# Loading k by two transfers, and leaving the second product of two blocks instead of four to the last phase, in a fused attention and feed-forward kernel

## The chip, the cores and the metric

The kernel runs on one core of one Trainium2 chip. Its engines each run their own in-order stream of instructions: TensorE (PE, matmuls, with its weight loads shown as PEld), VectorE (DVE), ScalarE (ACT), GpSimd (POOL) and SyncE (SP), whose queue issues nearly all of this kernel's DMAs. The metric is the device time of one execution in microseconds, the median of several runs. A profile is of one execution, and its "span" runs from the first to the last instruction.

## The reference

```python
def _attn_ref(q, k, v, f):                      # q, k, v: (8, 8, 576, 64); f: (8, 8, 576)
    scores = (1.0 / np.sqrt(D)) * np.matmul(q, k.transpose(0, 1, 3, 2))
    cum = np.cumsum(np.log(np.clip(f, 0.0001, 1.0)), axis=-1)
    scores = np.where(causal, -1000000000.0, scores + cum[..., :, None] - cum[..., None, :])
    attn = softmax of scores
    return np.matmul(attn, v)

def reference(...):
    x = attn_out.transpose(0, 2, 1, 3).reshape(B * S, H * D)     # 4608 tokens x 512
    h = x @ w_in                                                 # 512 x 2048
    g = np.maximum(h, 0.0) + np.log1p(np.exp(-np.abs(h)))        # softplus
    return g @ w_out                                             # 2048 x 512
```

So: causal attention with a cumulative decay for 8 batches of 8 heads, each with 576 tokens of 64 values, then a two-layer feed-forward network over the 4608 tokens. Below, "first product" is x @ w_in and "second product" is g @ w_out.

## The kernel before

**Numbers in two parts.** Most matmuls run on pairs: a value is cast to a high part in the engine's rounded float32 type, the rest (value minus high part) is the low part, and a product is high x high + high x low + low x high. So nearly every operand costs a cast (the copies recorded at L327, on ACT or DVE) and a subtraction (on DVE or POOL).

**Attention.** The eight heads of batch 0 are cut in 14 jobs in plain float32 (they fill the first stage, while weights are loaded). The other 56 heads (batches 1 to 7) are one job each, a "whole head". A whole head loads q, k and v (`load`, L881 to L895, and `load_v`), prepares them (`prepare`, L912: decay rows by DMA at L920 and L923, high parts of q and k by L927, low parts by L930 and L931), computes five tiles of scores (`stat_tile`: matmuls L976 and L977, row minimum L981, shift L1018, exponential L1025 on ACT), sums and scales (L1038 to L1055), turns the weights by matmuls into four banks (L1118) and splits them (L1137, L1140), and multiplies by v (L1265) into two banks that are put into x (L1315).

q and k are stored transposed: 64 rows of 576 values for each head. The kernel wants each in all 128 partitions, that is, twice. q is loaded by two transfers, one into partitions 0 to 63 and one into 64 to 127 (L886, 144 KB each). k is loaded by one transfer (L891, 288 KB) whose source pattern begins with a dimension of size 2 and stride 0, so that the 64 rows are read twice. Both go to buffers of the tag `raw`, of which there are two (L371); they alternate, and a buffer comes free when the cast and the subtraction that read it are done.

**Feed-forward blocks.** The first 2560 tokens are seven blocks (L360): 0 and 1 of 128 tokens, 2 of 256, and 3 to 6 of 512. A block's first product runs in 16 units (L1506, 12 matmuls of 512 columns each in a 512-token block), each followed by a softplus on ACT (`gate`, L1536). What comes then depends on the block. Blocks 0 and 1 run in plain float32 (L1485, L1618), and the sums of their second product hold one PSUM bank of tag `att` each. For block 2, the softplus tile is split into high and low parts (L1547, L1551) and multiplied by w_out straight away (`down_part`, L1608, matmuls in `products`, L1599) into two PSUM banks of the tag `att`. There are eight banks: two of tag `h` for the first product, six of tag `att` shared by scores, turned weights, outputs and these sums. For the blocks named in `LATE_DOWN` (3, 4, 5 and 6) the softplus tile is stored raw to DRAM (`raw_m`, two DMAs at L1567), and their second product waits for the last phase. A 512-token block that is not named there takes a third way, which no block takes before: the second product of its first two tiles of 128 tokens runs as units finish, the split parts of the other two tiles are stored (`keep`, L1555), and when the first two are done they are loaded again (`second`, L1646) and multiplied.

**The last phase.** The last 2048 tokens are two super-blocks of 1024, whose first product uses a scheme of seven products of halves in place of eight (L2071). After it comes the second product, by the same scheme, in "sets" of 42 matmuls of 256 columns: load (L2325), sums (L2345), splits (L2379), products (L2412). First the blocks of `LATE_DOWN` (8 sets each: 2 parts of 256 tokens x 4 quarters), then the super-blocks (16 sets each).

**The order.** The whole program is laid out when it is built. Each operation is added to a plan with the engines that can do it, an estimated cost, what it must follow and which buffers it takes. `Plan.run` (L205) then picks, again and again, the operation that can start first by these estimates, chooses its engine and emits it. That fixes each engine's stream; on the chip an instruction waits until what it needs is there, and everything behind it on its engine waits too. Two tables bend the choice: `SOONER` (L52) gives a kind of operation a head start in us, `RATHER` (L102) makes an engine look cheaper or dearer for a kind. Units of feed-forward work are dealt out between the units of attention (`run_ffn`, L2618) by a budget; in most whole heads a unit is dealt only once the budget has reached `PAIR` (L2739), 1.4 us, so they come in pairs.

Of the kernel before, what the change touches and what calls it, by code (L numbers as in the profile page):

```python
# [40 lines left out]
DELAY = 2  # L41
STEPB = -0.3
DEEP = 1
LATE_DOWN = (3, 4, 5, 6)
WSUMB = 0.0
DOWNB = 0.0
PAIR = 1.4

W_FROM, W_EACH = 0, 3
S_FROM, S_EACH = 9, 4  # L50

SOONER = {  # L52
    "attention.finish.put": 0.09,
    "attention.finish_stats.scale": -0.26,
    "attention.load.k": 0.17,
    "attention.output_tiled.values": 0.35,
    "attention.prepare.begin": -0.26,
    "attention.split_v.v_hi": -0.28,
    "attention.split_v.v_lo": 4.97,
    "attention.stat_tile.scores": 0.25,  # L60
    "attention.stat_tile.shift": 0.04,
    "attention.stat_tile.sums": 3.52,
    "attention.weights.keep": 0.05,
    "attention.weights.spread": -0.03,
    "decay.split": 6,
    "ffn_block.gate.lo_part": -0.02,
    "ffn_block.gate.whole_keep": -0.23,
    "ffn_block.split_stored.hi_part": 0.04,
    "ffn_block.split_stored.lo_part": 6,
    "ffn_block.split_stored.load": 6,  # L70
    "ffn_block.split_x.hi_part": -0.87,
    "joined.row": 0.28,
    "load_f64.clip": 0.25,
    "load_f64.join": 0.3,
    "load_f64.low": 0.32,
    "load_f64.scale": -0.22,
    "load_f64.sign": 0.32,
    "mark": -0.05,
    "put_out.<lambda>": 0.06,
    "set_rows.begin": -2.95,  # L80
    "split_w_in.keep": -0.52,
    "split_w_out.hi_part": -0.1,
    "store_x.store": -0.39,
    "super_blocks.down_out.keep": -0.06,
    "super_blocks.down_out.sum_.go": -0.2,
    "super_blocks.down_set.<lambda>": -0.67,
    "super_blocks.down_set.split.high": -0.28,
    "super_blocks.down_set.split.low": 0.03,
    "super_blocks.gate.store": -1.45,
    "super_blocks.hold_sums.begin": 5.59,  # L90
    "super_blocks.lay_sums.low": 0.15,
    "super_blocks.lay_w.split.hi": 1.29,
    "super_blocks.lay_w.split.lo": 0.23,
    "super_blocks.lay_w.step.go": 0.13,
    "super_blocks.lay_x.less.go": 0.28,
    "super_blocks.lay_x.split.high": -0.08,
    "super_blocks.lay_x.split.low": 1.61,
    "super_blocks.super_block.product.mm": -1.42,
    "super_blocks.super_block.ups.sum_of.go": 3.23,
    "turn_mask.turn": -1.48,  # L100
}
RATHER = {  # L102
    ("attention.finish_stats.scale", "DVE"): -0.98,
    ("attention.prepare.<lambda>", "ACT"): 0.02,
    ("attention.prepare.<lambda>", "DVE"): -0.18,
    ("attention.weights.hi_part", "DVE"): 1.11,
    ("attention.weights.keep", "ACT"): -1.02,
    ("attention.weights.keep", "DVE"): -1.85,
    ("attention.weights.spread", "ACT"): 0.73,
    ("ffn_block.gate.hi_part", "DVE"): 1.02,  # L110
    ("put_out.<lambda>", "DVE"): 0.72,
    ("split_w_in.hi_part", "DVE"): -1.77,
    ("split_w_out.hi_part", "DVE"): -2,
    ("super_blocks.down_set.split.high", "ACT"): -0.65,
    ("super_blocks.down_set.sum_.<lambda>", "DVE"): -0.83,
    ("super_blocks.lay_sums.<lambda>", "DVE"): -0.15,
    ("super_blocks.lay_sums.high", "ACT"): -1.79,
    ("super_blocks.lay_sums.low", "DVE"): -0.98,
    ("super_blocks.lay_w.split.hi", "DVE"): 1.26,
    ("super_blocks.lay_w.split.lo", "DVE"): -0.29,  # L120
    ("super_blocks.lay_x.split.high", "ACT"): 0.58,
    ("super_blocks.lay_x.split.high", "DVE"): 0.26,
}


def kind_of(emit):

    return emit.__qualname__.split("<locals>.", 1)[-1].replace("<locals>.", "")
# [15 lines left out]
class Plan:  # L144
# [14 lines left out]
    def add(self, on, emit, after=(), takes=(), lag=None, loose=False):  # L159
        op = Op(on, emit, after, takes, lag)  # L160
        op.loose = loose
        kind = kind_of(emit)
        op.sooner = SOONER.get(kind, 0.0)
        if len(op.on) > 1:
            op.on = [x._replace(bias=x.bias + RATHER.get((kind, x.eng), 0.0)) for x in op.on]
        op.at = len(self.ops)
        op.rank = op.at + self.late
        self.ops.append(op)
        for t in set(takes):
            self.queue[t].append(op)  # L170
        for d in op.after:
            d.users.append(op)
        return op

    def give(self, tag, ops):

        left = [len(ops), 0.0]
        for op in ops:
            self.gives.setdefault(op, []).append((tag, left))
# [78 lines left out]
def on_pe(n, times=1, m=128):  # L258

    return On("PE", times * (max(n * 0.000444, m * 0.00092) + 0.002))  # L260
# [20 lines left out]
def on_dma(kb, n=1, eng="SP"):  # L281

    return On(eng, max(0.6 * n, kb / RATE) if eng == "SP" else 1.5 * n)


def dma_lag(kb, n=1, eng="SP"):
    each = 0.6 if eng == "SP" else 1.5
    return each * (n - 1) + 2.1 + kb / n / RATE - on_dma(kb, n, eng).cost
# [26 lines left out]
def last_first(x, n=64):  # L315

    *lead, (_, w) = x.ap
    return bass.AP(x.tensor, x.offset + w - n, [*lead, [-n, w // n], [1, n]])
# [12 lines left out]
def tile_decay_attention_softplus_ffn(  # L331
# [39 lines left out]
                x32=2, ps=2, wl=2, vhl=3, vraw=1, raw=2, one=2)  # L371
    plan = Plan(BUFS | dict(T0=4, stat=4, p=2, xh0=1, xh1=1, xl0=1))
    add, give = plan.add, plan.give

    def joined():
        parts = []

        def row(e):
            for part in parts:
                part(e)  # L380

        op = add(On("PE", 0.0), row)
        op.parts = parts
        return op
# [11 lines left out]
    def add_dma(emit, kb, n=1, eng="SP", **more):  # L396
        return add(on_dma(kb, n, eng), emit, lag=dma_lag(kb, n, eng), **more)
# [9 lines left out]
    def buf(tag, shape, name, dtype=F32):  # L407
        return pool.tile(shape, dtype, tag=tag, name=name, bufs=BUFS[tag])
# [39 lines left out]
    raw_d = dpool.tile([NSUPER, 2, 2, SUPER // 256, 2, P, NFP // 2, P], F32, name="raw_d")  # L448
    raw_m = dpool.tile([len(LATE_DOWN), 2, 2, WIDE // 256, 2, P, NFP // 2, P], F32, name="raw_m")
    kept_at = {}  # L450
# [51 lines left out]
    def exchange(e):  # L502
# [12 lines left out]
            lambda e, x=x, v=v: e.mul(x, ident[0:BH, 0:BH], v) if e is nc.scalar  # L515
# [261 lines left out]
    def attention(job):  # L777

        b, heads = job["b"], job["heads"]
# [29 lines left out]
        st = {}  # L809
# [71 lines left out]
        def load():  # L881
            def q(e):
                st["q"] = buf("raw", [P, S], f"q{n}")
                for r in (0, 64):
                    out = st["q"][r : r + 64].rearrange("p (n t) -> p n t", t=64)
                    e.dma_start(out=out, in_=last_first(qkT[b, :, heads[0], 0]))  # L886

            def k(e):
                st["k"] = buf("raw", [P, S], f"k{n}")
                x = qkT[b, :, heads[0], 1]  # L890
                e.dma_start(out=st["k"], in_=bass.AP(x.tensor, x.offset, [[0, 2], *x.ap]))  # L891

            st["ql"] = add_dma(q, 288, 2, takes=("raw",))
            st["kl"] = add_dma(k, 288, takes=("raw",))

        def split_v():
            def v_hi(e):
# [427 lines left out]
        def loads():  # L1325
            if quad:
                load_quad()
            elif pair:
                st["T"] = T_of[heads[0]]
                st["vr"], st["V"], st["vtag"] = V_of[heads[0]]  # L1330
            else:
                (load32 if plain else load)()
                load_v()
# [53 lines left out]
    def ffn_block(i):  # L1387
# [148 lines left out]
        def gate(u):  # L1536
# [23 lines left out]
            give("h", [a])  # L1560
            if i in LATE_DOWN:
                m = LATE_DOWN.index(i)

# [129 lines left out]
        up_t, down_t = on_pe(nt, 6).cost, on_pe(DM, 3 * ahead).cost  # L1693
        raw_only = i in LATE_DOWN
        if plain:
# [33 lines left out]
    def super_blocks():  # L1729
# [704 lines left out]
        def down_out(s, k, out_box):  # L2434
# [4 lines left out]
            else:  # L2439
                t0 = BLOCKS[LATE_DOWN[s - NSUPER]][0]  # L2440
                rows = out[t0 : t0 + WIDE].rearrange("(t n) d -> t n d", t=2)
# [64 lines left out]
        sets = [  # L2506
            (NSUPER + m, k, q) for m in range(len(LATE_DOWN)) for k in range(WIDE // 256) for q in range(NQ)
        ]
# [109 lines left out]
    def run_ffn(budget, least=0.0):  # L2618
        if budget < least:
            return budget  # L2620
        while ffn and budget > 0:
            cost, unit = ffn.pop(0)
            plan.late = FFN_RANK
            unit()
            plan.late = 0
            budget -= cost
        return budget
# [49 lines left out]
    for n in range(len(jobs) + 1):  # L2677
# [58 lines left out]
        for unit in units:  # L2736
            unit()
            steady = n > nstart + H and (n - nstart) % H in (2, 3, 4, 5, 6)
            credit = run_ffn(credit + share, PAIR if steady else 0.0)  # L2739
        old = cur  # L2740
# [59 lines left out]
```

## Time and profile before

| | |
|---|---|
| three runs | 1365.43, 1368.46, 1370.01 us; median 1368.46 |
| the profiled execution | 1367.31 us, span 1365.2 us, mean granted TensorE clock 0.926 |
| busy in the span | PE 1185.0 us (87%), DVE 1011.4 (74%), ACT 813.7 (60%), POOL 387.1 (28%) |
| DMA | 204.83 MB, mean 150 GB/s; queue 1 takes 51.0% of 16 engines' time |
| HBM | 143.27 MB read, 59.93 MB written |

How to read the profile: its first part gives each engine's busy time; the second cuts the span in 40 equal slices with the busy share of each in tenths, the granted TensorE clock (PEclk) in tenths, and the DMA engines' mean busy share. The chain of waits is followed back from the last instruction: at each step to what released it. Groups of instructions are listed by source line, engine and tiles, as "out<-in", with count, busy time, mean ns of one, and the idle time of the engine just before them with what ended it. A line can be that of a helper: L327 is every copy and cast. A busy PE is not PE at its peak, since matmuls overlap and their ends are modelled: a matmul of 512 columns is shown as some 0.4 us long, while in a dense run the starts lie closer. The windows view gives the busy time of each engine in a stretch of the span, in us, with the number of instructions.

### The profile page before, as it was taken

How to read it: one execution, taken by the hardware profiler on the slowest of the kernel's cores; microseconds unless marked ns; L12 is line 12 of the kernel's file. 1: busy time of each engine (PE TensorE's matmuls, PEld its weight loads, DVE VectorE, ACT ScalarE, POOL GpSimd, SP SyncE). 2: the span in 40 equal slices, each digit the busy share in tenths (PEclk: the TensorE clock that was granted, in tenths of full speed). 3: DMA queues.
4: the chain of work that ended last, by engine and by line, in shares of the span. 5: the costliest groups of instructions: out<-in, count | busy, mean ns of one | idle time of the engine just before them, and what ended most of it. 6: DMA issues, size and time to landing. Idle time of an engine off the chain costs nothing.

```text
span 1365.2 us, 23032 instructions
## 1 busy us (share of the span) xinstructions
PE 1185.0 (87%) x7328; PEld 1029.5 (75%) x7328; DVE 1011.4 (74%) x2813; ACT 813.7 (60%) x2020; POOL 387.1 (28%) x356
## 2 busy tenths in 40 slices
PE   9998878788876678778777778999999999999998
PEld 7766667676765567566666567888788999999998
DVE  8997677667767476656665666765989988888884
ACT  6765756567766656666656667655666444444442
POOL 3334343234333343333433243021341111011010
PEclk9999888788888688987988898999999999999999
DMA  7875455344444334444444445787765444444442
GB/s 223 258 209 167 128 159 157 109 126 118 139 132 131 98 104 126 136 126 134 125 132 129 133 123 173 248 219 231 217 204 163 138 133 121 135 139 131 125 133 70
DMA packets 240058, 204.83 MB, mean 150 GB/s; under 512 B 85088, under 2 KB 208256, under 8 KB 239936
## 3 DMA queue, kind: packets, MB, share of 16 engines
q1 hardware_dynamic: 239912, 203.34, 51.0%
q8 instruction: 58, 0.95, 0.3%
q14 instruction: 64, 0.52, 0.1%
q10 hardware_dynamic: 24, 0.02, 0.0%
HBM read 143.27 MB, written 59.93 MB: 149 GB/s over the span
## 4 chain that ended last, share of the span: by engine, by line
PE 44%; DMA 33%; DVE 9%; ACT 5%; POOL 3%; issue 3%; SPq 2%; POOLq 0%; ACTq 0%; DVEq 0%
DMA k<-in_qkT 27%; PE late_E L2412 11%; PE late_E L2071 5%; PE late_B L2412 3%; PE late_D L2412 3%; PE late_C L2412 3%; PE late_A L2412 3%; PE h L1506 3%; POOL T L931 2%; DMA vr<-in_vR 2%; ACT T L327 2%; DMA wi_d<-woh_dt_float 2%; PE late_C L2071 2%; PE late_D L2071 2%; PE b L1118 1%
## 5 line engine op out<-in xcount | busy, mean ns | idle before, releaser
L976 PE MATMUL s<-T 128*128 128x192 f32 (+1 forms) x336 | 110.9, 340 | 76.9 <-DVE pl L1140 31.6
L1265 PE MATMUL o<-ph,vhl 128*128 128x512 f32 x336 | 108.8, 346 | 70.6 <-ACT p L1025 66.3
L931 POOL TENSOR_TENSOR T<-k,T 64x576 fp32r<-64x576 f32 x56 | 80.5, 1438 | 284.1 <-ACT T L327 142.9
L1025 ACT ACTIVATE pb<-s,negm 128x288 f32<-128x288 f32 (+5 forms) x272 | 142.6, 527 | 23.2 <-DVE negm L1018 19.5
L981 DVE CUSTOM_DVE_ANT_0 s<-s,cmask 128x448 f32<-128x448 f32 (+6 forms) x320 | 134.3, 445 | 23.6 <-PE s L977 19.3
L1265 PEld LDWEIGHTS o<-ph,vhl 128*128 128x128 f32 x336 | 74.4, 225 | 90.0 <-ACT p L1025 78.0
L976 PEld LDWEIGHTS s<-T 128*128 128x128 f32 (+1 forms) x336 | 67.2, 200 | 99.2 <-DVE pl L1140 38.2
L327 ACT CAST T<-k 64x576 fp32r<-64x576 f32 (+1 forms) x91 | 59.4, 671 | 128.0 <-DMA k<-in_qkT 128.0
L1315 DVE TENSOR_TENSOR x<-o,x 64x64 f32<-64x64 f32 x112 | 50.7, 455 | 98.8 <-ACT x L327 97.7
L1140 DVE TENSOR_TENSOR pl<-b,ph 128x512 fp32r<-128x512 f32 x168 | 105.0, 658 | 10.7 <-ACT ph L327 9.5
L977 PE MATMUL s<-T 68*128 68x192 f32 (+1 forms) x336 | 105.6, 318 | 0.0
L327 ACT CAST ph<-b 64x128 fp32r<-64x128 f32 x224 | 100.3, 486 | 6.0 <-PE b L1118 4.9
L1506 PE MATMUL h<-xh,wl 128*128 128x512 f32 (+1 forms) x320 | 101.8, 406 | 0.0
L931 POOL TENSOR_TENSOR T<-q,T 64x576 fp32r<-64x576 f32 x56 | 80.2, 1432 | 59.3 <-PE b L1118 24.6
L1506 PE MATMUL h<-xh,wih 128*128 128x512 f32 (+1 forms) x320 | 92.2, 415 | 1.4 <-ACT xh L327 1.4
L1118 PE MATMUL b<-halves,pb 128*128 128x128 f32 x512 | 91.5, 301 | 0.0
L1506 PE MATMUL h<-xl,wih 128*128 128x512 f32 (+1 forms) x320 | 88.5, 403 | 0.0
L903 POOL TENSOR_TENSOR vhl<-vr,vhl 128x384 fp32r<-128x384 f32 x56 | 56.8, 1015 | 102.5 <-DVE vhl L327 53.4
L1025 ACT ACTIVATE p<-s,negm 128x192 f32<-128x192 f32 (+1 forms) x112 | 40.5, 362 | 66.6 <-DVE negm L1018 66.2
L1265 PE MATMUL o<-pl,vhl 128*128 128x512 f32 x224 | 78.1, 397 | 0.1
L2345 POOL TENSOR_TENSOR fY<-fX,late_ph 128x256 f32<-128x256 f32 x13 | 10.4, 800 | 231.6 <-ACT late_pl L327 142.0
L977 PEld LDWEIGHTS s<-T 68*128 68x128 f32 (+1 forms) x336 | 68.2, 203 | 7.5 <-issue 1.8
(703 smaller groups left out, 3732.5 us busy)
## 6 DMA issues: line engine op xcount, KB each, us to landing
wl<-wil_d SPq DMA_DIRECT2D x40, 512.0 KB
raw_m<-e SPq DMA_DIRECT2D x128, 128.0 KB
raw_d<-e SPq DMA_DIRECT2D x64, 256.0 KB
q<-in_qkT SPq DMA_DIRECT2D x112, 144.0 KB
k<-in_qkT SPq DMA_DIRECT2D x56, 288.0 KB
vr<-in_vR SPq DMA_DIRECT2D x64, 160.0 KB
x_d<-x SPq DMA_DIRECT2D x28, 288.0 KB
late_r<-wi_d SPq DMA_DIRECT2D x14, 512.0 KB
```

The lines of the kernel that those rows point to most:

```text
L327: (e.tensor_copy if hasattr(e, "tensor_copy") else e.copy)(out, in_)
L931: e.tensor_sub(t[rows, i, :], st[x][rows], tb[rows, j, :])
L976: e.matmul(o, qA[:, S - end : S - q0], kA[:, a:z], start=True, stop=False)
L977: e.matmul(o, qB[0:ST, S - end : S - q0], kB[0:ST, a:z], start=False, stop=True)
L981: e.tensor_tensor_reduce(out=box["o"], in0=box["o"], in1=cmask[0:n_q, right - w : right], scale=-0.125, scalar=m0 if i else 3.0e38, op0=AL ...
L1025: e.activation(o, box["o"], AF.Softplus, bias=m1, scale=-1.0, accum_out=acc)
L1118: e.transpose(box["ps"][0 : x.shape[1], at : at + one.shape[1]], x, one)
L1140: e.tensor_sub(box["l"], box["ps"][:, 0:w], box["h"].bitcast(F32))
L1265: e.matmul(boxes[gi]["ps"][0:m, a:z], st["vhl"][:, c, 0:m], pbox[which][:, o : o + z - a], start=gi in fresh and which == "h", stop=gi == ...
L1506: e.matmul(o, l, r, start=m == 0, stop=m == 11)
L2071: e.matmul(banks[to], stationary(x, j), at(b, y, j), start=start and m == 0, stop=m == 5, skip_group_check=not start,)
L2412: e.matmul(like(o, y), x, y, start=q == 0 and f_ == 0 and m == 0, stop=q == NQ - 1 and f_ == 1 and m == 2,)
```

## The change

Three things change.

1. k is loaded by two transfers of 64 rows, as q is, in place of one of 128 rows with a repeating source. The plan is told that it is two.
2. `LATE_DOWN` is (5, 6) in place of (3, 4, 5, 6). Blocks 3 and 4 compute their second product in the middle (the third way above), and the last phase has two blocks fewer.
3. `PAIR` is 0.0 in place of 1.4, and the two tables are new: `SOONER` has 58 entries in place of 48 and `RATHER` 23 in place of 20, nearly all with other values. (`kind` also gets a suffix from an attribute `phase`, which nothing sets.)

```diff
-LATE_DOWN = (3, 4, 5, 6)
+LATE_DOWN = (5, 6)
 WSUMB = 0.0
 DOWNB = 0.0
-PAIR = 1.4
+PAIR = 0.0
...
 SOONER = {
-    "attention.finish.put": 0.09,
-    "attention.finish_stats.scale": -0.26,
-    "attention.load.k": 0.17,
...
+    "attention.finish_stats.scale": -0.13,
+    "attention.load.q": 0.09,
+    "attention.load32.qk": 4.25,
...
 RATHER = {
-    ("attention.finish_stats.scale", "DVE"): -0.98,
-    ("attention.prepare.<lambda>", "ACT"): 0.02,
...
+    ("attention.finish_stats.scale", "ACT"): -0.62,
+    ("attention.finish_stats.scale", "DVE"): -0.94,
...
-        kind = kind_of(emit)
+        kind = kind_of(emit) + getattr(self, "phase", "")
...
             def k(e):
                 st["k"] = buf("raw", [P, S], f"k{n}")
-                x = qkT[b, :, heads[0], 1]
-                e.dma_start(out=st["k"], in_=bass.AP(x.tensor, x.offset, [[0, 2], *x.ap]))
+                for r in (0, 64):
+                    e.dma_start(out=st["k"][r : r + 64], in_=qkT[b, :, heads[0], 1])

             st["ql"] = add_dma(q, 288, 2, takes=("raw",))
-            st["kl"] = add_dma(k, 288, takes=("raw",))
+            st["kl"] = add_dma(k, 288, 2, takes=("raw",))
```

More of the change, by code (lines that the diff above doesn't have):

```diff
@@ L52 @@
 SOONER = {
-    "attention.finish.put": 0.09,
-    "attention.finish_stats.scale": -0.26,
-    "attention.load.k": 0.17,
[L56 to L60, printed above, removed]
-    "attention.stat_tile.shift": 0.04,
[L62 to L72, printed above, removed]
-    "load_f64.clip": 0.25,
[L74 to L81, printed above, removed]
@@ L82 @@
-    "split_w_out.hi_part": -0.1,
-    "store_x.store": -0.39,
[L84 to L100, printed above, removed]
+    "attention.finish_stats.scale": -0.13,
+    "attention.load.q": 0.09,
+    "attention.load32.qk": 4.25,
+    "attention.load32.rows": 3.94,
+    "attention.output_tiled.put": 0.2,
+    "attention.prepare.<lambda>": -0.12,
+    "attention.prepare.decay_rows": 6,
@@ new lines @@
+    "attention.split_v.v_hi": -0.01,
+    "attention.split_v.v_lo": -0.07,
+    "attention.stat_tile.scores": 0.13,
+    "attention.stat_tile.shift": 0.04,
+    "attention.stat_tile.sums": 2.24,
+    "attention.weights.keep": -0.21,
+    "attention.weights.spread": -0.84,
+    "attention.weights.turn": 0.04,
+    "decay.<lambda>": -0.09,
+    "decay.store": 0.98,
+    "ffn_block.gate.hi_part": -0.02,
+    "ffn_block.gate.keep": 0.99,
+    "ffn_block.gate.lo_part": 0.01,
+    "ffn_block.gate.raw": -0.09,
@@ new lines @@
+    "ffn_block.split_stored.hi_part": 0.05,
+    "ffn_block.split_stored.lo_part": 5.53,
+    "ffn_block.split_stored.load": 5.04,
+    "ffn_block.split_x.hi_part": -0.12,
+    "ffn_block.up_part.load": 0.15,
+    "joined.row": 0.25,
+    "load_f64.clip": 0.25,
+    "load_f64.join": 0.17,
+    "load_f64.low": 0.24,
+    "mark": 0.07,
+    "put_out.<lambda>": -0.63,
+    "put_out.begin": -1.19,
+    "set_rows.<lambda>": 0.63,
+    "set_rows.begin": 3.55,
+    "split_w_in.hi_part": 0.03,
+    "split_w_in.keep": -0.37,
@@ new lines @@
+    "split_w_in.lo_part": -0.05,
+    "split_w_out.hi_part": -0.47,
+    "split_w_out.lo_part": -0.09,
+    "store_x.store": -0.39,
+    "super_blocks.down_products.mm": -2.57,
+    "super_blocks.down_set.<lambda>": -1.84,
+    "super_blocks.down_set.split.high": -0.24,
+    "super_blocks.gate.store": -0.66,
+    "super_blocks.lay_out.sums": 0.07,
+    "super_blocks.lay_sums.high": -0.59,
+    "super_blocks.lay_w.<lambda>": -0.92,
+    "super_blocks.lay_w.split.hi": 0.39,
+    "super_blocks.lay_w.split.lo": 3.36,
@@ L101 @@
+    "super_blocks.lay_w.step.go": 0.09,
+    "super_blocks.lay_x.load": -0.26,
+    "super_blocks.lay_x.split.high": -0.15,
+    "super_blocks.lay_x.split.low": 0.29,
+    "super_blocks.super_block.product.mm": -1.71,
+    "super_blocks.super_block.ups.moved.<lambda>": -0.8,
+    "super_blocks.super_block.ups.sum_of.go": -0.08,
+    "turn_mask.turn": -1.39,
 }
 RATHER = {
-    ("attention.finish_stats.scale", "DVE"): -0.98,
-    ("attention.prepare.<lambda>", "ACT"): 0.02,
-    ("attention.prepare.<lambda>", "DVE"): -0.18,
@@ L106 @@
[L106 to L122, printed above, removed]
+    ("attention.finish_stats.scale", "ACT"): -0.62,
+    ("attention.finish_stats.scale", "DVE"): -0.94,
+    ("attention.finish_stats.scale", "POOL"): -0.12,
+    ("attention.prepare.<lambda>", "ACT"): 0.4,
@@ new lines @@
+    ("attention.prepare.<lambda>", "DVE"): 0.26,
+    ("attention.split_v.v_hi", "ACT"): -0.39,
+    ("attention.split_v.v_hi", "DVE"): -1.23,
+    ("attention.weights.hi_part", "DVE"): 0.57,
+    ("attention.weights.keep", "ACT"): -1.5,
+    ("attention.weights.keep", "DVE"): -1.93,
+    ("ffn_block.gate.hi_part", "DVE"): -0.14,
+    ("ffn_block.gate.lo_part", "POOL"): -2,
+    ("load_f64.sign", "POOL"): -0.61,
+    ("set_rows.<lambda>", "DVE"): -2,
+    ("set_rows.<lambda>", "POOL"): -1.65,
+    ("split_w_in.hi_part", "ACT"): 1.76,
@@ L123 @@
+    ("super_blocks.down_set.split.high", "ACT"): 0.19,
+    ("super_blocks.down_set.split.high", "DVE"): -0.18,
+    ("super_blocks.down_set.sum_.<lambda>", "POOL"): 1.41,
+    ("super_blocks.lay_sums.<lambda>", "DVE"): -0.2,
+    ("super_blocks.lay_w.split.hi", "ACT"): 0.13,
+    ("super_blocks.lay_w.split.hi", "DVE"): 0.07,
+    ("super_blocks.lay_x.split.high", "ACT"): -1.28,
 }
```

## The prediction

> **What bounds the kernel now.** I read the page's head and slices first, then the busy time by stage, then the chain of waits of the long stage.
>
> ```profile
> span 1365.2 us, 23032 instructions
> ...
> PE   9998878788876678778777778999999999999998
> ...
> PEclk9999888788888688987988898999999999999999
> ```
> ```profile
> core 0: us, PE busy (x) PEld busy (x) DVE busy (x) ACT busy (x) POOL busy (x), PEclk, DMA share, GB/s
> 0.00:85.00 85.00, 82.52 (x560) 63.94 (x561) 75.40 (x249) 60.48 (x144) 29.79 (x55) 1.00 0.79 235
> 85.00:867.00 782.00, 613.15 (x3361) 508.25 (x3360) 527.18 (x1730) 510.20 (x1417) 283.08 (x227) 0.87 0.47 136
> 867.00:1059.00 192.00, 187.43 (x896) 155.63 (x895) 153.98 (x284) 110.48 (x214) 44.30 (x46) 1.00 0.73 210
> 1059.00:1365.00 306.00, 301.88 (x2516) 301.67 (x2514) 254.87 (x554) 132.58 (x247) 29.89 (x29) 1.00 0.41 125
> ```
>
> Three of the four stages are full: PE is busy 97%, 98% and 99% of them, at a granted clock of 1.00. The middle (85 to 867 us, the 56 whole heads and the blocks beside them) is not: PE 613.15 of 782 us (78%) at 0.87, DVE 67%, ACT 65%, POOL 36%. No engine fills it, so a chain of waits does. Its shares in that window, three of its pieces (start, length), and who waits for the loads from 85 to 838 us (total, times, longest):
>
> ```profile
> by line: DMA k<-in_qkT 47.9%; POOL T L931 4.2%; issue 3.9%; DMA vr<-in_vR 3.6%; ACT T L327 3.5%; PE h L1506 3.4%; DMA wi_d<-woh_dt_float 3.1%; DVE pl L1140 2.3%; SPq L886 2.2%; DVE s L981 2.1%; PE o L1265 2.0%; DMA sto<-in_w_out 2.0%; PE b
> ```
> ```profile
> 537.03 9.04 DMA k<-in_qkT
> 550.41 10.36 DMA k<-in_qkT
> 563.03 9.11 DMA k<-in_qkT
> ```
> ```profile
> ACT T L327 <- DMA k<-in_qkT: 128.0, 37, 5.9
> DVE T L327 <- DMA k<-in_qkT: 66.2, 17, 5.0
> ...
> DVE T L327 <- DMA q<-in_qkT: 2.0, 4, 0.7
> ```
>
> The load of k is 47.9% of 782, 375 us. One takes 9.04 to 10.36 us (mean of the three 9.50), and 54 of 56 are waited for, where q, as many bytes per head, is waited for four times. It is a ring: q and k share two raw buffers, so the k of the next head cannot be issued before this head's k or q has been cast and subtracted (L327, L931), and this head's k is late. From 537.03 to 550.41 to 563.03 is 13.4 and 12.6 us a head, and k's own flight is three quarters of it.
>
> **k by two transfers.** Two views show what the present transfer does. The DMA slices from 390 to 450 us, each 1.5 us, then the issues on SP and the cast of q on DVE:
>
> ```profile
> DMA  1346674111587715137257941136184117610231
> GB/s 52 120 118 191 156 230 118 51 51 51 135 153 271 238 58 159 52 111 240 100 131 128 311 123 51 53 105 143 31 236 158 51 51 197 223 53 9 57 127 51
> ```
> ```profile
> 548.33 1.33 SPq L886 DMA_DIRECT2D q<-in_qkT  x2
> 549.75 0.57 SPq L1477 DMA_DIRECT2D wl<-wil_d  x1
> 550.41 0.54 SPq L891 DMA_DIRECT2D k<-in_qkT  x1
> ...
> 553.12 4.67 SPq L920 DMA_DIRECT2D T<-aug_d  x1
> ```
> ```profile
> 552.81 0.46 DVE L327 CAST T<-q 128x576 fp32r<-128x576 f32 x1 [0.42 <-DMA q<-in_qkT]
> ```
>
> Again and again a slice stands at 1 tenth and 51 GB/s: about two of sixteen DMA engines work while little but k is in flight, and 295 KB at 51 GB/s are 5.8 of its 9.5 us. q, the same 295 KB in two transfers of 64 rows, is issued from 548.33 and the cast that waited for it starts at 552.81: 4.5 us for the pair. The new k has q's form (64 partitions each, one after the other), so I take 4.5, with the old 9.5 as the upper end and 3.8 as the lower (q's pair without the first issue, 1.33 / 2). [...]
>
> So 5.0 of 9.5 us go from each wait on the chain: 53% of 375 is 198 us, and 782 - 198 = 584 us is what the chain would leave if nothing else came late. It adds one issue per head at 0.54 us, 56 x 0.54 = 30 us of SP in 782; behind it on SP stand the value loads, the decay rows and the stores. I take zero for it: row L920 shows an issue that stood 4.67 us while k was in flight, which ends when k is spread; without that cover it costs 0.54 us a head where SP is late, 30 us at most. Transfers that use all engines also finish sooner once two of them are not held by k; that is in no term.
>
> **The second product of blocks 3 and 4 moves from the last phase to the middle.** Two pieces of chain give the pace, and two rows (busy and count over the whole span) the counts of L2412 and of L1599:
>
> ```profile
> 1143.44 1.44 PE late_E L2412 x12
> ```
> ```profile
> 270.84 1.36 PE acc L1599 x6
> ```
> ```profile
> 0.00:1365.00 1365.00, 323.89 (x2688) 323.02 (x2688) 0.93 0.51 150
> ```
> ```profile
> 0.00:1365.00 1365.00, 26.95 (x96) 17.78 (x96) 0.93 0.51 150
> ```
>
> Removed: the last phase has 64 sets (32 for the four blocks, 32 for the super-blocks) of 2688 / 64 = 42 matmuls at 1.44 / 12 = 0.120 us. Two blocks are 16 sets: 672 x 0.120 = 80.6 us. PE is busy 301.88 of 306 us there, so all of it leaves the span; the sets' loads, sums and splits go too and hide in it today. Added: 16 x 4 x 3 = 192 matmuls a block, 384 in all, at 1.36 / 6 = 0.227 us: 87 us of PE in the middle, beside it the split of 32 softplus tiles and eight copies out. The nearest rows for these:
>
> ```profile
> L327 ACT CAST late_w<-late_w 128x512 fp32r<-128x512 f32 (+1 forms) x32 | 16.4, 511 | 11.3 <-DMA late_w<-raw_d 6.0 <-DMA late_w<-raw_m 5.2
> ...
> L1140 DVE TENSOR_TENSOR pl<-b,ph 128x512 fp32r<-128x512 f32 x168 | 105.0, 658 | 10.7 <-ACT ph L327 9.5
> ```
>
> 32 x (0.511 + 0.658) + 8 x 0.511 = 41 us, shared by ACT and DVE: about 552 and 527 us of work there. In DMA, 2 x 32 raw stores become 2 x (28 stores, 14 loads, 4 outputs), 28 issues more, 15 us at 0.54, under the same cover.
>
> **The middle after it.** PE's work at full clock is 613.15 x 0.87 = 533, plus 87: 620 us, above the chain's 584, DVE's 552 and ACT's 527. So PE becomes the bound, and the question is how full it gets. The opening stage, same engines and no such k, reached 0.97 with DVE at 89%: 639 us. The stage where k is least on the chain today is this one, with its loads of k, a piece of its chain, and the same two rows for 390 to 500 us:
>
> ```profile
> 184.00:280.00 96.00, 77.82 (x460) 68.06 (x459) 72.31 (x211) 60.31 (x160) 31.21 (x24) 0.88 0.45 135
> 390.00:500.00 110.00, 76.39 (x389) 62.12 (x388) 74.31 (x250) 69.56 (x200) 45.82 (x33) 0.80 0.41 117
> ```
> ```profile
> k<-in_qkT SPq DMA_DIRECT2D x6, 288.0 KB
> ```
> ```profile
> k<-in_qkT SPq DMA_DIRECT2D x9, 288.0 KB
> ```
> ```profile
> 250.66 9.79 DMA wi_d<-woh_dt_float
> ```
>
> It reaches 0.81. The middle of 0.97 and 0.81 is 0.89; I take 0.90, since that stage also waits 9.79 us for copies that queue behind k. 620 / 0.90 = 689 us, 93 fewer. The new tables and the pair rule add no instruction. Outside the middle PE idles 2.5, 4.6 and 4.1 us, so a gain there is 11 us at most; a loss is bounded by no row, and I take zero. Inside it they are part of the 0.90.
>
> Sum: the profiled execution took 1367.31 us (span 1365.2). 1367.3 - 93 - 80.6 = 1193.7; the median of the three runs is 1.2 us above that execution, so **1195**.
>
> **The rivals.**
>
> *PE fills the middle as it fills the opening.* At 0.97 it lasts 639 us: 1367.3 - 143 - 80.6 = 1144, and with PE's true need below 533 (busy time counts overlapping matmuls) down to the chain's 584, 1089. For: ACT and DVE would need 82% and 86%, less than DVE's 89% there. Against: a whole head has a chain through all five engines.
>
> *The clock stays low.* At 0.87 the 620 us are 713, at 0.90 busy 792: ten more than now, 1367.3 + 10 - 80.6 = 1297. The granted clock is 1.00 wherever PE is 97% busy and lower only in the middle, where waits are long:
>
> ```profile
> PE o L1265 <- ACT p L1025: 63.5, 25, 5.7
> ```
>
> These are 25 waits of 2.5 us, up to 5.7, between 280 and 770 us. If they go and the clock does not recover, shorter gaps are enough to hold it. [...]
>
> *Slower: the two banks.* Blocks 3 and 4 each hold two of the six attention banks while their sums run. The stage from 184 to 280, in which block 2 held two, shows 96 / 6 = 16.0 us a head; 390 to 500, with none held, 110 / 9 = 12.2. After the change two thirds of the feed-forward work of the last 48 heads is such (87.2 + 87.2 of 262 us), 32 heads. With the other 24 at 689 / 56 = 12.3, it is slower once 32 x p + 295 exceeds 782 + 80.6: p above 17.7 us. At 18.5 the middle is 887, the total 1392. At the 16.0 seen it is 807 and 1312, still faster. Against: the opening stage held two banks as well, with PE at 97%.
>
> *The transfer does not spread.* If the halves still run on few engines, the ring stays 782 us and the 87 us of PE go into its 169 idle us: 1367.3 - 80.6 = 1287, up to 1374 if none hides.
>
> **How the numbers follow.** The forecast (1150 to 1260) has 0.70, a full middle 0.13, the low clock 0.08, the banks 0.05, no spread 0.04. The range from 1125 (PE busy without a gap, 620 us) to 1280 (0.80 busy, 775 us) leaves out the low clock, the banks, no spread and about 0.03 of the full middle. A measurement tells 0.3%, about 4 us, from no change: faster 0.94, the same 0.01, slower 0.05.
>
> **What would show it.** Right: k's pieces on the chain below 5 us or gone; no more runs of 51 GB/s slices; the middle 650 to 740 us long with PE 88 to 95% busy at 0.95 or more; 480 matmuls of the second product in the middle (L1599 now) and 2016 in the last phase (L2412 now), the latter some 242 us long. Wrong: k still on the chain at 9 us (the spread); the middle shorter than now but its clock below 0.92 (the clock); heads above 16 us where the middle's second product runs and waits of scores for banks (the banks); a last stage with idle PE (the order).

## The result and the profile after

The changed kernel takes 1149.88 us (median of 4 runs, 1147.93 to 1153.34) against 1369.24 for the kernel before (1365.43 to 1370.44): 0.8405 of it, 95% interval 0.8375 to 0.8435. That is 219 us less; the forecast was 174 less. 1149.88 lies in its range of 1125 to 1280, at the very edge of the 1150 to 1260 to which it gave 0.70.

The first lines of the page of the profile after, and the busy time by stage. The middle is counted from here on from 85 us to the first matmul of the super-blocks, at 878 us before and 740 us after; the second row pair is the same view of the kernel before, cut there.

```profile
span 1146.2 us, 22425 instructions
...
PE   9999998999999999999999999999899999999998
...
PEclk9999998999999999999999999999999999999999
```
```profile
core 0: us, PE busy (x) PEld busy (x) DVE busy (x) ACT busy (x) POOL busy (x), PEclk, DMA share, GB/s
0.00:85.00 85.00, 81.34 (x559) 64.02 (x559) 72.86 (x237) 56.76 (x148) 39.19 (x66) 1.00 0.78 229
85.00:740.00 655.00, 630.27 (x3788) 528.67 (x3788) 547.07 (x1753) 538.35 (x1463) 318.52 (x255) 0.99 0.62 180
740.00:1146.00 406.00, 397.43 (x2692) 368.12 (x2690) 328.21 (x699) 188.13 (x360) 65.62 (x62) 1.00 0.53 161
```
```profile
85.00:878.00 793.00, 624.15 (x3410) 517.38 (x3409) 533.83 (x1742) 514.89 (x1426) 283.08 (x227) 0.87 0.48 138
878.00:1365.00 487.00, 478.30 (x3361) 448.18 (x3359) 402.20 (x823) 238.38 (x452) 74.19 (x74) 1.00 0.52 156
```

The middle lost 138 us and the last phase 81; the opening stage is the same. In the middle PE now does more in less time: it is busy 630 of 655 us (96%, 79% before) at a clock of 0.99 (0.87 before). Busy time times clock, as an estimate of PE's work, gives 624.15 x 0.87 = 543 before, 630.27 x 0.99 = 624 after, the 87 us of the moved second product within rounding of the clock.

The chain's shares in that middle, its first piece, the one load of k among its longest pieces, and all waits of casts for the load of k (total, times, longest):

```profile
by line: PE h L1519 6.9%; ACT pb L1038 3.2%; DVE pl L1153 3.1%; DVE s L994 2.4%; PE o L1278 2.2%; issue 1.5%; PE acc L1612 1.5%; ACT x L340 1.5%; PE b L1131 1.4%; DVE lsum L1051 1.0%; DVE x L1328 0.9%; PE s L989 0.8%; DMA k<-in_qkT 0.8%; DM
...
507.49 0.49 ACT e L336
...
640.07 5.07 DMA k<-in_qkT
```
```profile
DVE T L340 <- DMA k<-in_qkT: 4.1, 4, 1.5
...
ACT T L340 <- DMA k<-in_qkT: 3.1, 5, 0.9
```

The casts' waits for k went from 54 of 194 us in all to 9 of 7 us. The chain agrees, with a reserve: here the profile can follow it back to 507 us only, so its shares of the 655 us cover the last 233. In these k has one piece of 5.07 us, 2%, where it had 47.9% before. Where its cast still waits, a flight can be read: issued from 386.09, cast from 391.09, five microseconds for the pair, one of the longer ones.

```profile
386.09 1.14 SPq L904 DMA_DIRECT2D k<-in_qkT  x2
```
```profile
391.09 0.46 DVE L340 CAST T<-k 128x576 fp32r<-128x576 f32 x1 [1.06 <-DMA k<-in_qkT]
```

The DMA slices of 390 to 450 us no longer show the runs of 1 tenth at 51 GB/s:

```profile
DMA  9920799423186867598486663401998427804432
GB/s 310 340 77 0 161 209 316 145 92 88 47 296 162 230 219 227 146 320 168 196 190 204 203 193 107 184 12 39 231 254 285 154 97 162 227 5 117 163 125 87
```

### The profile page after: what moved, and what is told of

It reads as the page before. It is cut to its first block, busy times and chain, and to the rows that moved or that the text cites. A ratio compares the mean times of both kernels' runs of the same rounds, so it can differ in the third digit from the quotient of the medians.

```text
span 1146.2 us, 22425 instructions
## 1 busy us (share of the span) xinstructions
PE 1109.0 (97%) x7036; PEld 960.8 (84%) x7036; DVE 948.1 (83%) x2687; ACT 783.2 (68%) x1968; POOL 423.3 (37%) x382
## 4 chain that ended last, share of the span: by engine, by line
PE 38%; DVE 9%; ACT 5%; DMA 2%; issue 1%; SPq 0%; POOL 0%; DVEq 0%; ACTq 0%
PE late_E L2425 10%; PE late_E L2084 5%; PE h L1519 4%; PE late_A L2425 3%; PE late_B L2425 3%; PE late_D L2425 2%; PE late_C L2425 2%; ACT pb L1038 2%; DVE pl L1153 2%; PE late_D L2084 2%; PE late_C L2084 2%; PE late_A L2084 2%; DVE s L994 1%; PE o L1278 1%; DMA late_x<-x_d 1%
## 5 line engine op out<-in xcount | busy, mean ns | idle before, releaser
L994 DVE CUSTOM_DVE_ANT_0 s<-s,cmask 128x320 f32<-128x320 f32 (+6 forms) x320 | 134.9, 442 | 20.2 <-PE s L990 16.3
L1519 PE MATMUL h<-xh,wl 128*128 128x512 f32 (+1 forms) x320 | 92.9, 377 | 0.0
L1278 PE MATMUL o<-ph,vhl 128*128 128x512 f32 x336 | 88.8, 300 | 2.7 <-ACT p L1038 1.5
L1519 PE MATMUL h<-xh,wih 128*128 128x512 f32 (+1 forms) x320 | 82.1, 378 | 0.0
L1131 PE MATMUL b<-halves,pb 128*128 128x128 f32 x512 | 80.6, 273 | 0.0
L1566 POOL TENSOR_TENSOR gl<-e,gh 128x512 fp32r<-128x512 f32 x40 | 52.5, 1312 | 61.9 <-DVE gh L340 24.5
L1278 PEld LDWEIGHTS o<-ph,vhl 128*128 128x128 f32 x336 | 62.2, 190 | 10.1 <-DVE pl L1153 3.2
L1278 PE MATMUL o<-pl,vhl 128*128 128x512 f32 x224 | 66.9, 346 | 0.0
L1519 PEld LDWEIGHTS h<-xl,wih 128*128 128x128 f32 x320 | 57.2, 190 | 10.9
L2392 POOL TENSOR_TENSOR late_ph<-late_ph,late_pl 128x256 fp32r<-128x256 f32 x10 | 10.4, 1042 | 149.8 <-DVE fX L2358 84.4
```

Source lines behind the costliest of these rows:

```text
L994: e.tensor_tensor_reduce(out=box["o"], in0=box["o"], in1=cmask[0:n_q, right - w : right], scale=-0.125, scalar=m0 if i else 3.0e38, op0=AL ...
L1131: e.transpose(box["ps"][0 : x.shape[1], at : at + one.shape[1]], x, one)
L1278: e.matmul(boxes[gi]["ps"][0:m, a:z], st["vhl"][:, c, 0:m], pbox[which][:, o : o + z - a], start=gi in fresh and which == "h", stop=gi == ...
L1519: e.matmul(o, l, r, start=m == 0, stop=m == 11)
```

## The experiments

Two theories went into them. The ring: k's slow flight, in a ring over two buffers, set the length of the middle, and the rest of the change matters only by how full the freed middle gets. Its rival, the order: the new tables and the pair rule, or the moved second product, brought the gain. Each median stands against the kernel before in the same set of runs (1362.4, 1362.4 and 1359.1 us in the three sets); differences under 1% between kernels of different sets are not told apart here, since the kernel before itself moved by 0.7% from set to set (1369.24 to 1359.1).

**k alone** (e1_k_only): the kernel before with

```diff
-                x = qkT[b, :, heads[0], 1]
-                e.dma_start(out=st["k"], in_=bass.AP(x.tensor, x.offset, [[0, 2], *x.ap]))
+                for r in (0, 64):
+                    e.dma_start(out=st["k"][r : r + 64], in_=qkT[b, :, heads[0], 1])
...
-            st["kl"] = add_dma(k, 288, takes=("raw",))
+            st["kl"] = add_dma(k, 288, 2, takes=("raw",))
```

> The kernel before with k loaded by two transfers and nothing else changed. If k's flight was the ring that set the middle (my theory), the middle falls from 793 us (85 us to the first matmul of the super-blocks at 878) to PE's 533 us of work at 0.90 to 0.96 busy, 555 to 590 us, the last phase stays: 1165 to 1200 us. If the new order (tables, pair rule) or the moved second product brought the gain, it stays above 1330.

1172.85 us, 0.8616 (0.8587 to 0.8644). Its middle:

```profile
85.00:683.00 598.00, 556.70 (x3405) 463.83 (x3404) 519.00 (x1730) 510.57 (x1420) 303.65 (x241) 0.98 0.64 182
683.00:1170.00 487.00, 478.81 (x3361) 448.23 (x3359) 401.90 (x823) 238.97 (x453) 74.57 (x74) 1.00 0.52 156
```

598 us for 793 (8 more than the 555 to 590 expected), the last phase unchanged to the microsecond. The edit brings 190 of the 219 us, and the clock comes back with it (0.98) with the old tables. It is not k's flight alone, though: the plan, told of two transfers, lays the work out anew (POOL has 241 instructions in the middle, where it had 227). The next run and the one with 62 rows keep the order of every compute engine.

**All but k** (e2_old_k): the changed kernel with the old load of k, its cost in the plan left at two transfers, so that the order is the same.

```diff
-                for r in (0, 64):
-                    e.dma_start(out=st["k"][r : r + 64], in_=qkT[b, :, heads[0], 1])
+                x = qkT[b, :, heads[0], 1]
+                e.dma_start(out=st["k"], in_=bass.AP(x.tensor, x.offset, [[0, 2], *x.ap]))
```

> The changed kernel with k loaded by one transfer with a repeating source, same costs in the plan and so the same order. Ring: the middle goes back to 780 to 860 us (k's flight, with 87 us more PE work in its gaps), the last phase keeps its 82 us: 1280 to 1360. Order: it stays below 1200, since everything else is the new kernel's.

1335.61 us, 0.9807 (0.9779 to 0.9836). The middle and the chain in it:

```profile
85.00:927.00 842.00, 700.79 (x3791) 581.58 (x3791) 552.06 (x1755) 543.77 (x1465) 315.28 (x255) 0.90 0.47 140
```
```profile
by line: DMA k<-in_qkT 41.9%; PE h L1519 8.3%; PE acc L1612 3.9%; PE o L1278 3.8%; POOL T L944 3.5%; DMA vr<-in_vR 3.4%; issue 3.3%; PE b L1131 2.7%; ACT T L340 2.6%; PE s L989 2.4%; DVE pl L1153 2.1%; PE s L990 1.9%; DMA q<-in_qkT 1.4%; DV
```

With the slow k all the rest of the change is worth 2% and not 16. k's flight as the main cause holds; the order as the main cause is out. The next run reaches the same time with the moved second product alone, so with a slow k the new order adds nothing.

**The moved second product alone** (e3_late_only): the kernel before with

```diff
-LATE_DOWN = (3, 4, 5, 6)
+LATE_DOWN = (5, 6)
```

> The kernel before with only blocks 5 and 6 left to the last phase. Ring: the 87 us of PE work hide in the 169 us that PE idles in the middle, and the last phase loses 82: 1285 to 1310. If they do not hide: 1367 + 87 - 82, 1370 or more. If two PSUM banks fewer lengthen the heads beyond that: over 1390.

1334.33 us, 0.9799 (0.9768 to 0.983), more than the 1285 to 1310 that I expected. The middle is 838 us, 45 more than before, and the last phase 407, 80 less: of 87 us of PE work about half hid in 169 us of idle PE. Here idle time beside a chain of waits was not free room. That the added work delays the chain where it stands in front of a head's scores is the likely reason; no run shows it.

**k and the moved product, old order** (e4_k_and_late): both edits, tables and pair rule as before.

> The kernel before with k by two transfers and blocks 5 and 6 alone left to the last phase; tables and pair rule as before. If the tables and the pair rule only order what already fits, 1150 to 1180, near the changed kernel's 1150. If they carry a share of the gain, more than 1190.

1188.00 us, 0.8713 (0.8679 to 0.8746): between the two expectations, next to the one in which the tables carry a share, and slower than k alone. The middle:

```profile
85.00:783.00 698.00, 655.24 (x3803) 545.02 (x3802) 563.87 (x1783) 542.67 (x1456) 306.49 (x243) 0.96 0.59 170
```

The moved product adds 100 us to the middle (598 to 698) and takes 79 from the end. (The profiled run is the slowest of the four, 5 us above the median.) 655.24 x 0.96 = 629 us of PE work in 698 us is 0.90 of full clock: the value that the prediction took, reached by the old order. The new order brings it to 624 / 655 = 0.95, which is 43 us.

**The tables or the pair rule** (e8_pair, the changed kernel with `PAIR = 1.4`; e9_k_late_pair0, the previous kernel with `PAIR = 0.0`).

> The changed kernel with the pair rule back at 1.4 us. New tables and pair rule together brought 38 us over k and the moved products alone (0.8713 to 0.8405). If the pair rule carried that: 1175 to 1195. If the tables did: 1145 to 1160.

> The kernel before with k by two transfers, blocks 5 and 6 alone left to the last phase and the pair rule at 0, old tables. The other side of the same question: 1150 to 1165 if the pair rule carried it, 1180 to 1195 if the tables did.

1154.84 us, 0.8477 (0.8441 to 0.8513), and 1176.82 us, 0.8634 (0.859 to 0.8679). With old tables the pair rule brought 11 us (1188.00 to 1176.82; the intervals just touch), with new ones 5 (1154.84 to 1149.88, two sets, so not certain). The tables brought 33 us with the old pair rule (1188.00 to 1154.84) and 27 with the new one (1176.82 to 1149.88), again across sets. The first run lies where it should if the tables carry the gain (1145 to 1160), the second in neither range, 3 us below the tables' 1180: the tables have the larger share, the pair rule at most a third.

**Four blocks late again** (e7_late_four): the changed kernel with `LATE_DOWN = (3, 4, 5, 6)`.

> The changed kernel with blocks 3 to 6 left to the last phase again. With the old tables the move of blocks 3 and 4 cost 15 us once k was fast (ratio 0.8713 against 0.8616). If the move is a loss whatever the order, since the middle has become full and takes eight products for seven: middle 533 / 0.95 = 561 to 598 us, 1125 to 1165. If the new tables were fitted to the moved products and lose without them: 1170 or more.

1171.08 us, 0.8595 (0.8558 to 0.8633), k alone within the intervals. So the new order gains nothing without the moved product (10 us in the middle, which the last phase, 8 us longer than with k alone, gives back), and the moved product loses (15 us) without the new order; together they bring some 21 us. The middle of this kernel:

```profile
85.00:673.00 588.00, 551.06 (x3410) 463.23 (x3408) 502.48 (x1699) 514.31 (x1435) 309.15 (x252) 0.98 0.66 186
```

With less for PE to do, PE, DVE and ACT stand at 94%, 85% and 87%. That three engines so full at once keep it from getting shorter is likely, but was not tried. The 87 us of PE work more needed 67 us more of time there (588 to 655) and saved 89 in the last phase (495 to 406).

**One block more in the middle** (e10_late_one): `LATE_DOWN = (6,)` in the changed kernel.

> The changed kernel with block 5's second product in the middle as well, only block 6 left to the last phase. Two blocks moved there cost the middle 57 us (598 to 655 us, new tables) and took 82 off the end. If the middle still has that room: 1135 to 1142. If PE, busy 96% of it at a clock of 0.99, is its bound now, the move costs 43.5 us there and takes 40.3 from the end: 1150 to 1165.

1155.77 us (1148.95 to 1158.99), 0.8503 (0.8458 to 0.8548), no gain: 6 us above the changed kernel, in another set. In the profiled run, the fastest of the four and 7 us below their median, the middle is 695 us, 40 more, and the rest 367, 39 less: the exchange is at its end.

```profile
85.00:780.00 695.00, 670.14 (x3971) 561.28 (x3970) 564.76 (x1770) 545.90 (x1459) 328.70 (x260) 1.00 0.60 175
780.00:1147.00 367.00, 356.84 (x2355) 327.52 (x2353) 296.57 (x626) 174.31 (x334) 62.46 (x58) 1.00 0.54 164
```

**Few engines, or the repeating source?** (e5_rows_62_2) The changed kernel with each half of k in two plain pieces:

```diff
                 for r in (0, 64):
-                    e.dma_start(out=st["k"][r : r + 64], in_=qkT[b, :, heads[0], 1])
+                    for a, z in ((0, 62), (62, 64)):
+                        e.dma_start(out=st["k"][r + a : r + z], in_=qkT[b, a:z, heads[0], 1])
```

> The changed kernel with each half of k loaded in two pieces, 62 rows and 2 rows: four plain transfers, no repeating source, same order of the work. What made the old load slow: its few DMA engines, or its repeating source and being one big transfer? [...] Few engines: k takes 9 us again and the time is that of the old load in the new kernel, 0.98 of before, 1315 to 1360 us. Repeating source: 1150 to 1165 (two issues more per head).

1358.23 us, 0.9966 (0.9939 to 0.9994). The whole gain is gone with no repeating source and no big transfer. In its middle k is back on the chain; of three of its pieces two show k's length:

```profile
by line: DMA k<-in_qkT 41.8%; PE h L1520 7.3%; PE acc L1613 4.0%; issue 4.0%; SPq L905 3.9%; PE o L1279 3.7%; POOL T L945 3.4%; ACT T L340 2.8%; DVE pl L1154 2.3%; PE s L990 2.0%; PE b L1132 1.6%; PE s L991 1.4%; SPq L899 1.3%; DMA g_d<-gh 
```
```profile
396.41 8.14 DMA k<-in_qkT
408.22 9.10 DMA wl<-wil_d
423.30 8.93 DMA k<-in_qkT
```

From the first issue to the last landing a head's k takes 9.5 us by the median, where the old load takes 9.23 and the changed kernel's pair 3.9. So a repeating source is not needed for the slow load. SP's time for issuing k is the same (70 us in all, 65 in the changed kernel), so the two issues more per head are not the cause. The 23 us that it takes beyond e2 stay open.

What is left is the number of rows in a transfer: in two pieces of 64 a head's k lands in 3.9 us, in pieces of 62 and 2 in 9.5. That 62 rows run on few engines, as the expectation takes it, was the author's estimate. The landing records (the signals on a transfer's semaphore) tell the loads apart: a transfer of k gives 3 signals here and in the kernel before, and 16 in the changed kernel. In the kernel before, one of the three comes 0.96 us after the issue and the other two at 8.87 and 9.23 (medians). How many engines stand behind them no run shows; about two of sixteen is the prediction's estimate, from the slices at 51 GB/s. `wl`, which gives 16 signals, takes 9.10 us in the second piece, where its median in the changed kernel is 4.48; that it waits there behind k is a guess that was not tried.

**A third buffer** (e14_control_raw2 and e13_raw3_old_k): does the slow flight cost because two raw buffers close it into a ring? To make room for a third, a control first gives up one buffer of `fe` and one of `one`; the next kernel adds the raw buffer. Both are the kernel before, with its old load of k.

```diff
-    BUFS = dict(T=2, att=6, h=2, fe=4, ...
-                x32=2, ps=2, wl=2, vhl=3, vraw=1, raw=2, one=2)
+    BUFS = dict(T=2, att=6, h=2, fe=3, ...
+                x32=2, ps=2, wl=2, vhl=3, vraw=1, raw=3, one=1)
```

> The kernel before with one buffer fewer of two small tags (fe 3 for 4, one 1 for 2), to pay for the next kernel's third raw buffer: the same as before or some us slower, 1360 to 1385.

> That control with three raw buffers for two, k still by one transfer with the repeating source. If the slow flight costs because the two buffers make it a ring, a third lets the next k start before this head's k has been used: below its control by 30 us or more, 1250 to 1345. If the two loaded DMA engines are the bound themselves (two transfers of k cannot fly side by side on them), or the order of casts holds the buffers anyway: within 10 us of its control.

The control took 1375.41 us, 1.0128 (1.0088 to 1.0168); with the third buffer 1344.28, 0.9897 (0.9856 to 0.9937). That is 31 us less, 25 of them in the middle (790 to 765). The chain's shares from 310 us to the end of the middle, the part that the chains of both runs cover, control first:

```profile
by line: DMA k<-in_qkT 50.5%; PE h L1506 4.9%; POOL T L931 4.4%; ACT T L327 4.3%; DMA vr<-in_vR 3.9%; issue 3.4%; DMA raw_m<-e 3.4%; PE b L1118 2.8%; PE o L1265 2.4%; SPq L886 2.1%; DMA wl<-wil_d 1.8%; DMA late_x<-x_d 1.3%; ACT pb L1025 1.2
```
```profile
by line: DMA k<-in_qkT 46.9%; PE h L1506 9.0%; PE o L1265 3.7%; DMA vr<-in_vR 3.5%; POOL T L931 3.5%; issue 3.4%; ACT T L327 3.2%; DVE pl L1140 3.2%; DMA q<-in_qkT 2.0%; DVE T L327 1.9%; DVE s L981 1.9%; PE s L976 1.6%; PE b L1118 1.6%; PE 
```

The two buffers cost something, but a third does not take k off the chain, and half of q now lands 8.57 us after its issue (median), where it took 3.32 in the control. Each of the two kernels is laid out anew by the plan, so the 31 us are not surely the buffer's alone. Against the 190 us that k by two transfers brings, they say that most of the cost is in the flight itself.

**The other load with a leading repeat of 2** (e12_v_spread): the changed kernel with the last 64 rows of v loaded by two transfers. By one transfer, in the changed kernel, they too give 3 landing signals, the last 3.38 us after the issue (median).

```diff
-                        twice = bass.AP(x.tensor, x.offset, [[0, 2], *x.ap])
-                        e.dma_start(out=vr[:, NCH], in_=twice)
+                        for r in (0, 64):
+                            e.dma_start(out=vr[r : r + 64, NCH], in_=x)
```

> The changed kernel with the other repeating source cured too: the last 64 rows of v, 32 KB that go to both halves of the partitions by one transfer with a leading dimension of 2, loaded by two transfers. Few engines cost only where a head waits for the transfer: v is 0.8% of the chain now, so 1147 to 1153, the same. If few engines hold up others' transfers: down to 1135. If SP's issues are late: over 1155.

1152.53 us (1151.95 to 1154.86), 0.8491 (0.8453 to 0.8529): as expected no gain; this load is not what a head waits for.

No version here beats the changed kernel.

## Why the prediction was right, step by step

*k's load as the bound of the middle: right,* shown by all but k (0.98) and by 62 rows (0.9966), in which every compute engine runs the changed kernel's order, and by k alone (190 of 219 us). *As a ring over two buffers: shown only in part,* since a third buffer brought 31 us and left k on the chain.

*The new flight, 4.5 us for the pair: right in size.* Where it can be read in a cast's wait it is 5 us; the landing records (issue to last signal) give 3.26 us as the median of one half, 0.6 us after the other, and 3.9 us for the pair. They also show what the prediction put in no term: other transfers got shorter, by their medians the weights of the first product from 6.53 to 4.48 us, v from 6.72 to 2.80, the copies of w_in from 7.90 to 3.55.

*What k would still cost: too much, without effect on the sum.* The prediction left 375 - 198 = 177 us of k on a chain of 584. With k alone, where the profile follows the chain through the whole middle, k has 2.4% of 598 us, 14 us:

```profile
by line: PE h L1506 13.4%; DVE s L981 8.8%; DVE pl L1140 8.2%; ACT pb L1025 8.0%; issue 5.5%; PE b L1118 5.2%; PE o L1265 5.0%; DVE lsum L1038 3.2%; ACT x L327 2.8%; PE s L976 2.5%; DMA k<-in_qkT 2.4%; DMA q<-in_qkT 2.3%; ACT ph L327 2.3%; 
```

Where k landed before it was wanted, it was not shortened on the chain but left it. PE's 620 stood above the 584, so the forecast did not change by it.

*SP's extra issues at zero: right.* The cover named was an issue that stood 4.67 us behind k. Here is that line (min, median, max in ns) before and after. Added up over the trace, the issues of k went from 30 to 65 us and those of the decay rows (this line and the next) from 124 to 32, so the faster ones gave back more than the issues more for k cost.

```profile
L920 SPq DMA_DIRECT2D T<-aug_d x56: 228/558/5010, 92.2 to 835.1; - x56
```
```profile
L933 SPq DMA_DIRECT2D T<-aug_d x56: 233/260/697, 80.6 to 689.2; - x56
```

*The last phase, 80.6 us less: right* (487 to 406), with 2016 matmuls in 242.94 us of busy time (and 480 of the second product in the middle, as forecast).

```profile
0.00:1146.00 1146.00, 242.94 (x2016) 242.26 (x2016) 1.00 0.60 177
```

*PE as the new bound with 620 us of work: right.* 624 by the same product of busy time and clock, where the longer middle counted here would make it 543 + 87 = 630.

*How full the middle gets, 0.90: the term that was mis-sized.* Measured 0.95 (624 of 655). At 0.90 the middle as counted here would last 630 / 0.90 = 700 us, and the 45 us to 655 are those by which the forecast was too slow. The 0.90 is what the old order reaches (e4), in part by luck: it was picked between the rows of two other stages. The step that failed is "The new tables and the pair rule add no instruction ... Inside it they are part of the 0.90". They add none, but with the moved product in the middle they are worth 38 us (1188.00 to 1149.88, in two sets; 0.8713 to 0.8405), which the prediction did not count. The opening stage's 0.97 was the better row to go by, the stage from 184 to 280 us the worse, since its 0.81 was the slow k's too. With k alone the same stretch, which then holds 72 of the 96 matmuls of block 2's second product, has PE busy 0.93 of it at full clock:

```profile
184.00:280.00 96.00, 88.91 (x559) 75.49 (x558) 86.46 (x280) 83.55 (x230) 57.07 (x44) 1.00 0.59 169
```

*The moved second product as a plain exchange: right only with the new order.* With the old order it loses 15 us behind a fast k, and behind a slow k it hides half and not all.

*The rivals.* The full middle (1144, chance 0.13) was the nearest, 6 us off, where the forecast's 1195 was 45 off. Two banks did not decide: in the changed kernel from 390 to 500 us, with the second product running, stand 18 halves of k, 9 heads, 12.2 us a head and far from 17.7.

```profile
k<-in_qkT SPq DMA_DIRECT2D x18, 144.0 KB
```

The low clock did not stay (0.99), but e4 shows a fall to 0.50, below. No spread is what e5 comes to, with k at 9.5 us, and its 1358 lies in the 1287 to 1374 given for it.

## What to carry to other kernels

When a transfer stands on the chain far longer than a sibling of the same bytes, look at its shape before its size: here k took 9.23 us with a leading dimension of 2 and 9.5 in pieces of 62 and 2 rows, against 3.9 in two pieces of 64 rows, and the fix is two lines. Idle time beside such a load was only in part room for other work until the load was cured (half of 87 us); what the room is worth shows only afterwards. And when an engine becomes the bound, the order of its work can be worth some per cents (38 us here), so it has to be fitted after the cut: here the moved product paid only under the new order, and the new order only with the moved product.

## What the runs showed of the hardware that was not expected

The clock fell without any long wait. In e4, four windows around 715 us:

```profile
700.00:714.00 14.00, 10.55 (x62) 7.68 (x60) 12.45 (x43) 11.12 (x31) 7.72 (x6) 1.00 0.58 167
714.00:716.00 2.00, 1.13 (x6) 0.83 (x7) 1.91 (x9) 1.33 (x5) 0.36 (x1) 0.71 0.95 226
716.00:732.00 16.00, 14.12 (x52) 11.58 (x51) 11.19 (x32) 10.09 (x29) 7.47 (x6) 0.50 0.54 187
732.00:740.00 8.00, 8.00 (x39) 6.63 (x38) 4.82 (x11) 4.66 (x14) 3.79 (x2) 1.00 0.59 151
```

Up to 714 us PE was busy 75% in short pieces at a granted clock of 1.00. Then the clock fell to 0.50, and it was back at 1.00 from 732 us, after PE had been busy 88% of the 16 us before. The longest gap of PE from 700 us to the fall is 1.01 us, in front of this matmul:

```profile
703.33 0.40 PE L976 MATMUL s<-T 128*128 128x288 f32 x1 [1.01 <-DVE pl L1140]
```

So the gaps before the fall were small; whether they brought it, no run here shows.
